# High and low log decays in one operand, and a new fixed order for the first tile of a three-stage kernel

## The chip, the cores and the metric

The kernel runs on one core of a Trainium2 chip. The metric is the device time of one execution in microseconds. The engines are PE (TensorE, matrix products; PEld is its loading of weights), DVE (VectorE), ACT (ScalarE), POOL (GpSimd) and SP (SyncE, which here issues every DMA).

## What is computed

A decaying linear attention over 4 x 8 heads and 768 positions in chunks, then two feed-forward stages on its 3072 x 256 output:

```python
log_a = np.log(np.clip(a, 1e-06, 1.0))
for c in range(nc):                                   # chunks
    cum = np.cumsum(la, axis=-1)
    L = np.exp(cum[:, :, :, None] - cum[:, :, None, :]) * causal
    M = np.einsum('bhin,bhjn->bhij', Cc, Bc) * L
    y[:, :, sl] = einsum(M, xc) + einsum(Cc, state) * exp(cum)
    state = exp(sum(la)) * state + sum_j(Bc[j] xc[j] * decay_from_j)
x = attn.transpose(0, 2, 1, 3).reshape(3072, 256)
x = (np.maximum(x @ w_in, 0.0) ** 2) @ w_out          # 256 -> 2048 -> 256
y = ((x @ w1) * (x @ w2) @ w3) @ w_out2               # 256 -> 1024 -> 1024 -> 256
```

The inputs are float32 (the weights arrive as 64-bit words that hold float64).

## The kernel before

The 3072 tokens are cut into six tiles of 512. Phase A of a tile is the first feed-forward stage (16 steps: `h_mm`, ReLU, square, `x2_mm`), phase B the second (8 steps). A value that enters a product of full accuracy is split into a high part, rounded to float32r, and a low part, the rest (`split`: ACT casts, DVE subtracts, L141 and L144), and a product is made of three passes over the parts.

**Weights.** A weight piece of 512 KB is fetched by `conv_load` (`ua0`, `ua1`, ... for the first stage) and converted: `conv_words` on ACT (L196, L198), `conv_bits` on DVE (L207, L210), `conv_parts` a cast on ACT for the first three pieces (L230) and on POOL for the others (L228), with the low part on DVE (L141). In the first tile's phase A one piece is converted in each of the 16 steps.

**Attention.** Chunks of 96 positions come in units of two. Units 0 to 2 (chunks 0 to 5), which the first tile needs, are computed in `startup()`, in an order written out by hand; every engine keeps it. For them `unit_g0` makes C.B on PE (L620), `unit_e1` the log decays as products of a selecting operand `pick` with `e_first` (L652), on top of a mask product (L646), and ACT takes their exponential (L656); `unit_m0` multiplies the two on DVE (L664). `state` and `value` are products on PE (L702, L740), and their results go over ACT and DVE to `xb` of the next chunk and to `xt`, the first tile's operand. From unit 3 on, `unit_split` splits B and C on ACT and DVE and writes them to DRAM (`hl_d`), and `unit_bc` reads them back in another layout with twelve DMAs (`bt`, `cb`).

**e_first** holds the cumulated log decays of the first two batches, for four kinds of chunk, in 32-row blocks. It is made by `decays_e_first` from the log decays `lp` and two shifted copies `lp2`, and kept as a high and a low half: every pick is made of two products, one per half, accumulated in PSUM. Four pick products follow each mask product.

**Order.** `startup()` runs under `in_order`, which ties each instruction to the one before it on its engine. Behind it a scheduler places the instructions of phase A and B. DMAs go out on SP in the order of the program, and SP waits in that order: a DMA that must wait holds back the ones behind it.

Of the kernel before, what the change touches and what calls it, by code (L numbers as in the profile page):

```python
# [15 lines left out]
P = 128  # L16
# [32 lines left out]
WARM = 2  # L49
TMPB = 6  # L50
# [3 lines left out]
PAD_ACT = (1, 2)  # L54
# [4 lines left out]
def kernel(  # L59
# [226 lines left out]
    lp2 = lps[:, 192:256].rearrange("p (v c) -> p v c", v=2)  # L286

    def constants():
        def diagonal(v):
            nc.gpsimd.affine_select(  # L290
                out=v, in_=v, pattern=[[0, v.shape[1]], [-1, v.shape[2]]], base=0, channel_multiplier=1,
                compare_op=ALU.not_equal, fill=1.0,
            )
# [5 lines left out]
        nc.vector.memset(lp2, 0.0)  # L299
        raw = [new_tmp()[:, :P] for _ in range(2)]  # L300
        nc.gpsimd.memset(raw[0], 0.0)
        diagonal(raw[0].unsqueeze(1))
        nc.gpsimd.memset(raw[1][:, :CH], 0.0)
        causal(raw[1][:, :CH].unsqueeze(1), NEVER)
        for k, eng in enumerate((nc.vector, nc.gpsimd)):
            eng.tensor_copy(
                pick[k].rearrange("r h (p j) -> r h p j", p=4),
                raw[0].rearrange("r (p k h) -> r k h p", p=4, k=4)[:, k].unsqueeze(3).to_broadcast([P, H, 4, 32]),
            )
        nc.vector.tensor_copy(ident, raw[0])  # L310
        nc.vector.tensor_copy(nmask, raw[1][:, :CH])
        nc.gpsimd.memset(id2, 0.0)
        for p in range(4):
            diagonal(id2[32 * p:32 * p + 32].unsqueeze(1))
        nc.gpsimd.memset(idc, 0.0)
        diagonal(idc[96:128])
        nc.gpsimd.memset(bt[64:96, :, :, CH:].bitcast(F32), 0.0)
# [10 lines left out]
    def decays_ln():  # L328
# [958 lines left out]
```

## Time and profile before

| | us |
|---|---|
| runs, median (lowest to highest) | 575.24 (574.53 to 681.34) |
| the profiled execution, its own time | 575.9 |
| its span in the trace | 574.2 |
| PE busy | 555.4 (97%) |
| DVE busy | 359.4 (63%) |
| ACT busy | 291.2 (51%) |
| POOL busy | 86.5 (15%) |

The shares are means over the whole span; the first 107 us look different from the rest. The trace gives for each instruction its start and duration, its line, what it writes and reads, and the idle time of its engine just before it with what ended that. A count such as x4 merges neighbours of one kind; where a merged row covers instructions that overlap, its duration is that of the whole group.

### The profile page before, as it was taken

The page shows a single profiled execution, that of the slowest core. Times are in us where ns is not written, and L with a number is a line of the kernel's source. Part 1 is how long each engine was busy: PE and PEld are TensorE (multiplying, and loading weights), DVE is VectorE, ACT ScalarE, POOL GpSimd, SP SyncE. Part 2 cuts the span into 40 slices and gives each one's busy share as a digit, 9 for nine tenths or more (in the row PEclk, how much of TensorE's full clock was granted, in tenths as well). Part 3 has the DMA queues.
Part 4 walks back from the last instruction along what each step waited for, and adds up shares of the span by engine and source line. Part 5 has one row for each costly group of instructions (what it writes and reads, how often), then busy time and mean ns, then how long its engine had stood idle before and what let it go on. Part 6 is the DMA issues. An engine that isn't in the chain of part 4 may idle for free.

```text
span 574.2 us, 9685 instructions
## 1 busy us (share of the span) xinstructions
PE 555.4 (97%) x3612; PEld 466.1 (81%) x3612; DVE 359.4 (63%) x647; ACT 291.2 (51%) x560; POOL 86.5 (15%) x134
## 2 busy tenths in 40 slices
PE   8878889999999999999999999999999999999997
PEld 6666667788888888888888888888888888888886
DVE  5558989888899675455766455665466574544431
ACT  6659776878887333352533353433454242534332
POOL 6315652000000304003012004020003020000000
PEclk9978999999999999999999999999999999999999
DMA  8268878034254635028241037220063220100001
GB/s 238 66 198 269 240 238 346 1 111 156 71 182 148 160 112 142 1 87 196 82 113 56 1 116 179 61 77 2 8 171 87 82 70 1 38 1 1 0 2 37
DMA packets 48735, 59.49 MB, mean 104 GB/s; under 512 B 22960, under 2 KB 36784, under 8 KB 48688
## 3 DMA queue, kind: packets, MB, share of 16 engines
q1 hardware_dynamic: 48688, 58.88, 35.4%
q8 instruction: 28, 0.46, 0.3%
q14 instruction: 19, 0.16, 0.1%
HBM read 50.20 MB, written 8.65 MB: 103 GB/s over the span
## 4 chain that ended last, share of the span: by engine, by line
PE 84%; DMA 8%; DVE 3%; ACT 2%; SPq 2%; issue 1%; DVEq 0%; ACTq 0%
PE mm L804 42%; PE acc L851 19%; PE acc L904 12%; PE mm L257 4%; DMA ua<-in_w_dram 3%; PE y L740 2%; SPq L93 2%; DMA hl_d<-gp 2%; PE g L601 2%; DMA uo<-in_w_dram 1%; PE y L702 1%; PE mm L652 1%; DMA hl_d<-hl 1%; DMA u<-in_w_dram 1%; PE mm L646 1%
## 5 line engine op out<-in xcount | busy, mean ns | idle before, releaser
L804 PE MATMUL mm<-xt,wa 128*128 128x512 f32 x576 | 150.5, 399 | 3.9 <-DVE wa L141 2.3
L834 ACT CAST gp<-tmp 128x512 fp32r<-128x512 f32 x144 | 89.4, 621 | 114.7 <-DVE tmp L892 62.7
L851 PE MATMUL acc<-gp,wa 128*128 128x512 f32 x576 | 146.0, 392 | 0.7 <-DVE gp L141 0.4
L804 PE MATMUL mm<-x,w 128*128 128x512 f32 x576 | 142.6, 393 | 0.0
L141 DVE TENSOR_TENSOR gp<-tmp,gp 128x512 fp32r<-128x512 f32 x144 | 101.5, 705 | 64.2 <-ACT gp L834 63.7
L804 PEld LDWEIGHTS mm<-xt,wa 128*128 128x128 f32 x576 | 106.8, 192 | 28.0 <-DVE wa L141 4.5
L851 PEld LDWEIGHTS acc<-gp,wa 128*128 128x128 f32 x576 | 106.4, 188 | 24.1 <-DVE gp L141 1.8
L804 PEld LDWEIGHTS mm<-x,w 128*128 128x128 f32 x576 | 104.5, 188 | 20.4 <-ACT tmp L884 0.2
L818 ACT ACTIVATE tmp<-mm 128x512 f32<-128x512 f32 x96 | 57.1, 596 | 55.7 <-PE mm L804 55.4
L904 PEld LDWEIGHTS acc<-w3o,gp 128*128 128x128 f32 x576 | 75.9, 190 | 4.8 <-DVE gp L141 0.5
L904 PE MATMUL acc<-w3o,gp 128*128 128x256 f32 x576 | 78.7, 283 | 0.1
L828 DVE TENSOR_TENSOR tmp<-tmp 128x512 f32<-128x512 f32 x68 | 47.3, 697 | 29.8 <-ACT tmp L818 29.4
L892 DVE TENSOR_TENSOR tmp<-tmp,mm 128x512 f32<-128x512 f32 x48 | 32.9, 686 | 48.3 <-PE mm L804 45.5
L536 POOL TENSOR_SCALAR_AFFINE_SELECT e<-e 96x768 f32<-96x768 f32 x26 | 26.2, 1019 | 238.9 <-DMA e<-e_d 135.1
L884 ACT COPY tmp<-mm 128x512 f32<-128x512 f32 x48 | 28.2, 587 | 46.3 <-PE mm L804 45.9
L555 POOL TENSOR_TENSOR xb<-xb,dec 96x256 f32<-96x256 f32 x32 | 22.7, 708 | 100.7 <-DMA xb<-in_xb_dram 44.2
L607 DVE TENSOR_TENSOR e<-g,e 128x384 f32<-128x384 f32 x52 | 27.7, 551 | 7.6 <-PE g L601 4.5
L257 PE MATMUL mm<-wo,w 128*128 128x256 f32 x128 | 23.7, 284 | 0.4 <-DVE w L141 0.4
L730 DVE SCALAR_TENSOR_TENSOR xb<-xb,through,y 32x64 f32<-32x64 f32 x72 | 20.4, 283 | 3.2 <-PE y L702 1.5
L257 PEld LDWEIGHTS mm<-wo,w 128*128 128x128 f32 x128 | 20.6, 191 | 2.0 <-DVE w L141 1.0
L207 DVE SCALAR_TENSOR_TENSOR cvs<-cvs,ua 128x512 uint32<-128x512 uint32 x16 | 13.1, 820 | 10.3 <-ACT ua L198 10.2
L601 PEld LDWEIGHTS g<-cb,bt 96*128 96x128 f32 x96 | 16.0, 190 | 2.6
(111 smaller groups left out, 462.4 us busy)
## 6 DMA issues: line engine op xcount, KB each, us to landing
u<-in_w_dram SPq DMA_DIRECT2D x24, 512.0 KB, 4.3
ua<-in_w_dram SPq DMA_DIRECT2D x16, 512.0 KB, 7.2
e<-e_d SPq DMA_DIRECT2D x40, 192.0 KB, 5.3
xb<-in_xb_dram SPq DMA_DIRECT2D x32, 192.0 KB, 4.3
bt<-hl_d SPq DMA_DIRECT2D x78, 48.0 KB, 2.0
hl_d<-gp SPq DMA_DIRECT2D x9, 384.0 KB, 2.5
cb<-hl_d SPq DMA_DIRECT2D x66, 48.0 KB, 2.0
out_dram<-tmp SPq DMA_DIRECT2D x10, 256.0 KB, 2.6
```

Of the source, the lines that this page charges most:

```text
L141: return nc.vector.tensor_tensor(out=lo, in0=src, in1=hi.bitcast(F32), op=ALU.subtract)
L257: nc.tensor.matmul(acc[:, :DM], v[:, l, e % 4 * P:(e % 4 + 1) * P], wo2[1 + e // 2][r][:, e % 2 * DM:(e % 2 + 1) * DM], start=(n == 0), st ...
L601: nc.tensor.matmul(ps[:, 2 * pp:2 * pp + 2], w, un["c2"][:, pr, :, j * CH:(j + 1) * CH], start=True, stop=True)
L607: nc.vector.tensor_tensor(out=m, in0=ps, in1=m, op=ALU.mult)
L804: i = nc.tensor.matmul(ps, w[m][:, l, col + k * P:col + (k + 1) * P], rhs[k][:, r, :], start=((l, r, k) == (1, 0, 0)), stop=((l, r, k) == ...
L818: nc.scalar.activation(r, ps, AF.Relu)
L828: nc.vector.tensor_tensor(out=g32, in0=r, in1=r, op=ALU.mult)
L834: nc.scalar.copy(g[:, 0, :], d[k])
L851: i = nc.tensor.matmul(acc["x2", t][e], wa[m][:, l, 256 + e * P:256 + (e + 1) * P], g[:, r, :], start=(m == 0 and n == 0), stop=(m == MF - ...
L884: nc.scalar.copy(s, ps)
L892: nc.vector.tensor_tensor(out=p32, in0=prods[t, m], in1=ps, op=ALU.mult)
L904: i = nc.tensor.matmul(acc["o"][sub // per][:, sub % per, :], g[:, l, sub * P:(sub + 1) * P], w3o[m // 2][:, r, m % 2, :], start=(m == 0 a ...
```

## The change

1. `lp4` takes the place of `lp2`: for each kind of chunk the 16 columns of log decays stand twice, side by side. `decays_e_first` then gives every row twice. The copies are two on ACT and four on DVE (before: four on ACT).
2. `e_first` is one 128-row operand: in the first of the two sets of rows minus the high part, in the other minus the low part. A `scalar_tensor_tensor` makes it in one operation from the rounded copy `e_hi` and PSUM, with the 0/1 column `halves[:, 1]` as the factor. `pick` selects both rows with -1. So a pick is one product.
3. The warm-up products read a 128-column fill and a broadcast column; `cb` is zeroed on POOL instead of DVE; the pick operands and constants come in another order. The pads of units 0 and 2 are on DVE (before: unit 0 alone), the copies into `bi` all on DVE.
4. `startup()` has another order. Unit 3 is split right behind the first two pick groups of unit 1, and weight 3 is loaded in the first block, weight 4 right behind unit 3's write.

```diff
-    lp2 = lps[:, 192:256].rearrange("p (v c) -> p v c", v=2)
+    lp4 = lps[:, 192:320].rearrange("p (v d c) -> p v d c", v=4, d=2)
...
-        warm = gp.tile([P, 512], F32, tag="gp", name="warm")
-        nc.vector.memset(warm, 0.0)
+        zero = gp.tile([P, P], F32, tag="gp", name="zero")
+        nc.vector.memset(zero, 0.0)
         for _ in range(WARM):
-            nc.tensor.matmul(y_bank, warm[:, :P], warm, start=True, stop=True, skip_group_check=True)
+            nc.tensor.matmul(
+                y_bank, zero, zero[:, :1].to_broadcast([P, 512]), start=True, stop=True, skip_group_check=True
+            )
...
+        nc.gpsimd.memset(cb.bitcast(F32), 0.0)
+        nc.gpsimd.memset(raw[:, :192 + CH], 0.0)
+        for base in (0, -16):
+            diagonal(sel, base, 32, -1.0)
...
+        def put(copy, v, r, r_in, k):
+            copy(lp4[r, v], lp[r_in, k, :2 * H].unsqueeze(1).to_broadcast([r.stop - r.start, 2, 2 * H]))
+
+        put(nc.scalar.copy, 0, slice(0, P), slice(0, P), 0)
+        put(nc.scalar.copy, 3, slice(0, P), slice(0, P), 2)
         for v, r, k, r_in in ((0, 64, 1, 0), (0, 32, 0, 96), (1, 0, 1, 64), (1, 64, 2, 0)):
             n = 32 if r == 32 or k == 2 else 64
-            nc.scalar.copy(lp2[r:r + n, v], lp[r_in:r_in + n, k, :4 * H])
+            put(nc.vector.tensor_copy, v + 1, slice(r, r + n), slice(r_in, r_in + n), k)
...
-        nc.scalar.copy(e_first[:, 0], pv)
-        nc.vector.tensor_tensor(out=e_first[:, 1], in0=pv, in1=e_first[:, 0].bitcast(F32), op=ALU.subtract)
+        hi = wts.tile([P, 4, CH], F32R, tag="wa11", name="e_hi")
+        nc.scalar.copy(hi, pv)
+        nc.vector.scalar_tensor_tensor(
+            out=e_first, in0=hi.bitcast(F32), scalar=halves[:, 1:2], in1=pv, op0=ALU.mult, op1=ALU.subtract
+        )
...
-            if u in PAD_ACT:
+            if u not in PAD_DVE:
...
         for h in range(2):
-            for l in range(2):
-                nc.tensor.matmul(
-                    ph[:, h], pick[k][:, 2 * q + h], e_first[:, l, v:v + 2], start=(not mask and l == 0), stop=(l == 1),
-                    skip_group_check=True,
-                )
+            nc.tensor.matmul(
+                ph[:, h], pick[k][:, 2 * q + h], e_first[:, v:v + 2], start=not mask, stop=True, skip_group_check=True
+            )
...
         unit_e1(1, 1)
-        conv_words(0)
-        conv_bits(0)
+        unit_split(3, "w120")
+        unit_rows(bt)
+        state(1)
+        chunk_pre(3)
         value(0)
...
+        conv_load(1)
+        unit_bc(3)
```

On SP, from the seventeenth DMA on, before the change (`raw` are a unit's operands, `ua` the weights, `hl_d3` and `hl_d4` the split operands of units 3 and 4 in DRAM, `xb` a chunk):

```order
L93 DMA raw_133<-in_raw_dram 128x2x192
L93 DMA ua2_135<-in_w_dram 128x1024
L93 DMA hl_d3_478<-hl_473 128x2x384
L93 DMA ua3_481<-in_w_dram 128x1024
L93 DMA raw_483<-in_raw_dram 128x2x64
L93 DMA raw_483<-in_raw_dram 128x2x32
L93 DMA bt_90<-hl_d3_478 32x4x96 x6
L93 DMA cb_91<-hl_d3_478 16x4x192 x6
L93 DMA xb_514<-in_xb_dram 96x512
L93 DMA ua4_516<-in_w_dram 128x1024
L93 DMA hl_d4_538<-hl_533 128x2x384
```

and at the same place with the change:

```order
L93 DMA ua2_133<-in_w_dram 128x1024
L93 DMA raw_135<-in_raw_dram 128x2x192
L93 DMA ua3_137<-in_w_dram 128x1024
L93 DMA hl_d3_328<-hl_323 128x2x384
L93 DMA ua4_392<-in_w_dram 128x1024
L93 DMA bt_90<-hl_d3_328 32x4x96 x6
L93 DMA cb_91<-hl_d3_328 16x4x192 x6
L93 DMA xb_493<-in_xb_dram 96x512
L93 DMA ua5_495<-in_w_dram 128x1024
L93 DMA raw_497<-in_raw_dram 128x2x64
L93 DMA raw_497<-in_raw_dram 128x2x32
L93 DMA hl_d4_508<-hl_503 128x2x384
```

Weight 3 now stands ahead of unit 3's write and weight 4 ahead of the twelve reads. From the thirtieth DMA on the two orders are alike.

On DVE, from the decay products of unit 0 (`e<-g,e`) to those of unit 2, before the change (`cvs` and `wa` are the conversion of weight 0, `xt` the low part of a value, `hl` that of unit 3's split):

```order
L664 TENSOR_TENSOR e<-g,e 128x2x192 x4
L207 SCALAR_TENSOR_TENSOR cvs<-cvs,ua_121 128x512
L210 SCALAR_TENSOR_TENSOR cvs<-ua_121,cvs 128x512
L141 TENSOR_TENSOR xt<-mm,xt 128x2x96
L664 TENSOR_TENSOR e<-g,e 128x2x192 x4
L141 TENSOR_TENSOR xt<-mm,xt 128x2x96 x2
L141 TENSOR_TENSOR wa_462<-cvs,wa_462 128x512
L664 TENSOR_TENSOR e<-g,e 128x2x192 x4
L141 TENSOR_TENSOR hl<-raw_111,hl 128x192
```

and with the change (L679 is the line of the decay products, L602 that of the pads):

```order
L679 TENSOR_TENSOR e<-g,e 128x2x192 x4
L141 TENSOR_TENSOR hl<-raw_111,hl 128x192
L141 TENSOR_TENSOR hl<-raw_113,hl 128x192
L141 TENSOR_TENSOR xt<-mm,xt 128x2x96
L602 TENSOR_SCALAR cp<-raw_113,halves 128x192 x2
L141 TENSOR_TENSOR xt<-mm,xt 128x2x96
L679 TENSOR_TENSOR e<-g,e 128x2x192 x4
L207 SCALAR_TENSOR_TENSOR cvs<-cvs,ua_121 128x512
L210 SCALAR_TENSOR_TENSOR cvs<-ua_121,cvs 128x512
L141 TENSOR_TENSOR xt<-mm,xt 128x2x96 x2
L679 TENSOR_TENSOR e<-g,e 128x2x192 x4
```

Unit 3's split and two pads moved ahead of the decay products of unit 1, where now two values stand instead of one; ahead of those of unit 2 the low part of weight 0 is gone.

## Rows read from the trace of the kernel before

**Rows 1.** Stretches: us; busy PE, PEld, DVE, ACT, POOL; clock; DMA; GB/s.
```profile
20.00:25.00 5.00, 4.53 (x76) 3.64 (x74) 0.67 (x2) 3.26 (x9) 1.75 (x4) 1.00 0.00 0
52.00:80.00 28.00, 25.40 (x148) 19.05 (x147) 27.95 (x42) 20.53 (x42) 19.52 (x23) 1.00 0.74 202
80.00:92.00 12.00, 9.42 (x61) 6.64 (x59) 9.04 (x19) 8.85 (x19) 4.38 (x6) 1.00 1.00 355
107.00:574.00 467.00, 462.82 (x2843) 395.01 (x2842) 278.50 (x503) 215.49 (x399) 42.26 (x60) 1.00 0.28 78
```

**Rows 2.** Chain that ended last: start, us, engine, tile, line, count.
```profile
8.31 0.38 PE mm L646
8.69 0.42 PE mm L652 x4
9.11 0.20 PE mm L646
...
10.36 0.86 PE g L620 x16
...
12.65 0.56 PE y L702 x8
...
14.01 0.47 PE mm L740 x16
```

**Rows 3.** Timeline of PE: start, us, line, operands, count [idle before <-releaser].
```profile
26.93 1.40 PE L740 MATMUL mm<-e,xb 128*32 128x96 f32 x32 [2.40 <-DVE e L664]
...
30.04 2.93 PE L804 MATMUL mm<-xt,wa 128*128 128x512 f32 x6 [0.94 <-ACT xt L144]
...
44.51 0.69 PE L652 MATMUL mm<-e_first,pick 128*128 128x192 f32 x4 [3.55 <-ACT e L656]
45.03 4.54 PE L804 MATMUL mm<-xt,wa 128*128 128x512 f32 x12
...
50.79 1.52 PE L804 MATMUL mm<-xt,wa 128*128 128x512 f32 x6
```

**Rows 4.** Timeline of DVE.
```profile
25.30 1.94 DVE L664 TENSOR_TENSOR e<-g,e 128x384 f32<-128x384 f32 x4
```

**Rows 5.** Timeline of ACT.
```profile
23.66 0.49 ACT L656 ACTIVATE e<-mm 128x384 f32<-128x384 f32 x1 [0.43 <-PE mm L652]
...
27.97 0.32 ACT L144 CAST xt<-mm 128x192 fp32r<-128x192 f32 x1 [1.90 <-PE mm L740]
...
29.29 0.59 ACT L144 CAST hl<-raw 128x192 fp32r<-128x192 f32 x2
...
35.52 0.59 ACT L818 ACTIVATE tmp<-mm 128x512 f32<-128x512 f32 x1
...
38.75 0.60 ACT L818 ACTIVATE tmp<-mm 128x512 f32<-128x512 f32 x1 [0.70 <-PE mm L804]
42.58 0.66 ACT L196 ACTIVATE cvs<-ua 128x512 f32<-128x512 f32 x1 [3.23 <-DMA ua<-in_w_dram]
```

**Rows 6.** Timeline of SP's queue of DMA issues.
```profile
27.80 0.39 SPq L93 DMA_DIRECT2D hl_d<-hl x1
...
32.42 2.72 SPq L93 DMA_DIRECT2D bt<-hl_d x6
...
38.57 0.43 SPq L93 DMA_DIRECT2D ua<-in_w_dram x1
```

**Rows 7.** Line 207 from 28 to 110 us: ns min/median/max, first and last start.
```profile
L207 DVE SCALAR_TENSOR_TENSOR cvs<-cvs,ua x15: 677/693/1358, 29.4 to 88.6; 128x512 uint32<-128x512 uint32 x15
```

**Rows 8.** DVE by line and shape, 0 to 30 us: busy us, mean ns | idle.
```profile
L141 DVE TENSOR_TENSOR xt<-mm,xt 128x192 fp32r<-128x192 f32 x5 | 1.8, 352 | 1.5 <-ACT xt L144 1.5
...
L296 DVE MEMSET warm<- 128x512 f32 x1 | 0.5, 485 | 1.0 <-PEq L1273 1.0
```

**Rows 9.** One-microsecond stretches of PE: us, busy, clock, DMA, GB/s.
```profile
28.00:29.00 1.00, 1.00 (x20) 0.52 0.27 100
...
45.00:46.00 1.00, 1.00 (x5) 0.55 1.05 315
```

More of the change, by code (lines that the diff above doesn't have):

```diff
@@ L49 @@
 WARM = 2
+PAD_DVE = (0, 2)
 TMPB = 6
@@ new lines, in constants @@
+        nc.vector.memset(lp4, 0.0)
+        raw = new_tmp()
+        sel, one, low = raw[:, :64].rearrange("r (p c) -> r p c", p=4), raw[:, 64:192], raw[:, 192:192 + CH]
+        nc.gpsimd.memset(cb.bitcast(F32), 0.0)
+        nc.gpsimd.memset(raw[:, :192 + CH], 0.0)
+        for base in (0, -16):
+            diagonal(sel, base, 32, -1.0)
+        diagonal(one.unsqueeze(1), 0, 0)
+        causal(low.unsqueeze(1), NEVER)
+        nc.gpsimd.memset(id2, 0.0)
+        for p in range(4):
+            diagonal(id2[32 * p:32 * p + 32].unsqueeze(1), 0, 0)
@@ L311, in constants, with rounded @@
[L311 to L317, printed above, removed]
+        def rounded():
+            nc.vector.tensor_copy(ident, one)
+            nc.vector.tensor_copy(nmask, low)
+        return picks, rounded
     def decays_load(k):
@@ L385, in decays_e @@
         e_rows[w] = e
-    e_first = wts.tile([P, 2, 4, CH], F32R, tag="w127", name="e_first")
+    halves = const.tile([P, 2], F32, name="halves")
+    e_first = wts.tile([P, 4, CH], F32R, tag="w127", name="e_first")
     def decays_e_first():
@@ L572 @@
     cps = {}
-    halves = const.tile([P, 2], F32, name="halves")
     def unit_pad(u):
@@ L1044, in value, with m0 @@
             chunk_out(g, ys[g])
+        def m0(u):
+            for q in range(4):
+                unit_m0(u, q)
         decays_load(0)
@@ L1061, in startup @@
         chunk_xb(5, "w126")
+        conv_load(1)
         unit_load(4)
         conv_load(1)
-        constants()
+        picks, rounded = constants()
         decays_ln()
-        nc.vector.memset(cb.bitcast(F32), 0.0)
-        decays_e_first()
+        picks(0, nc.vector)
+        rounded()
         nc.vector.tensor_reduce(
@@ L1070, in startup @@
         )
+        decays_e_first()
+        picks(1, nc.gpsimd)
         nc.vector.tensor_copy(bi[:, :, CH:], id2.unsqueeze(1).to_broadcast([P, FIRST[1], 32]))
@@ L1075, in startup @@
         chunk_pre(0)
+        for q in range(4):
+            unit_e1(0, q)
+        unit_g0(0)
         chunk_pre(1)
-        unit_e1(0, 0)
-        unit_e1(0, 1)
-        unit_e1(0, 2)
-        unit_g0(0)
-        unit_e1(0, 3)
-        for q in range(4):
-            unit_m0(0, q)
         unit_bi(2, 6)
         unit_pad(1)
+        state(0)
         chunk_pre(2)
+        m0(0)
         unit_e1(1, 0)
-        state(0)
         unit_e1(1, 1)
-        conv_words(0)
-        conv_bits(0)
+        unit_split(3, "w120")
+        unit_rows(bt)
+        state(1)
+        chunk_pre(3)
         value(0)
+        unit_pad(2)
         unit_e1(1, 2)
         unit_g0(1)
-        state(1)
         unit_e1(1, 3)
-        chunk_pre(3)
-        for q in range(4):
-            unit_m0(1, q)
         value(1)
+        m0(1)
+        conv_load(1)
+        unit_bc(3)
+        state(2)
+        chunk_pre(4)
+        conv_words(0)
         unit_e1(2, 0)
-        unit_pad(2)
-        state(2)
         unit_e1(2, 1)
-        chunk_pre(4)
+        conv_bits(0)
         value(2)
+        state(3)
+        chunk_pre(5)
+        unit_e1(2, 2)
         unit_g0(2)
-        unit_e1(2, 2)
-        state(3)
         unit_e1(2, 3)
-        conv_parts(0)
-        chunk_pre(5)
-        for q in range(4):
-            unit_m0(2, q)
-        unit_split(3, "w120")
-        unit_rows(bt)
-        conv_load(1)
-        unit_load(5)
-        unit_bc(3)
         value(3)
+        m0(2)
         state(4)
@@ L1123, in startup @@
         conv_load(1)
+        unit_load(5)
+        conv_parts(0)
+        unit_split(4, "w121")
         value(4)
+        chunk_xb(7)
+        conv_load(1)
         conv_words(1)
-        conv_bits(1)
-        unit_split(4, "w121")
-        chunk_xb(7)
-        conv_load(2)
         value(5)
         state(5)
+        conv_bits(1)
         chunk_xb(8)
```

26 lines of the change are left out of this document (10 added, 16 removed).

## The prediction

> **What bounds the kernel now.** I read the table by stretches first [rows 1]. From 107 us to the end PE is busy for 462.8 of 467 us at the full clock, and there the change leaves the order of every engine as it was: a microsecond gained or lost before that point is gained or lost at the end. The question is when the program reaches it. From 52 to 80 us DVE is the full engine (27.95 of 28 us); from 80 to 92 it is busy for 9.04 of 12 us and the DMA engines are at 1.00.
>
> Then I read the timelines of PE, DVE, ACT and SP up to 52 us [rows 3 to 6] for one long wait and followed it back. PE stands still for 3.55 us before 44.51, since ACT has not emptied a PSUM buffer. ACT stands for 3.23 us before 42.58, since weight 4 has not landed. That piece was issued at 38.57, behind twelve reads of unit 3's split operands that begin at 32.42; those wait for the write issued at 27.80, once DVE had made the split. Meanwhile, from 20 to 25 us, the DMA engines moved nothing [rows 1]. A second, smaller loss is the stretch from 80 to 92, where DVE has 2.96 us without work and the DMA engines have none to spare.
>
> **Up to the first tile's first product,** which stands at 30.04 [rows 3]. I lay the new order end to end.
>
> (a) The fill ahead of the warm-up products shrinks from 512 columns, 0.485 us [rows 8], to 128; in proportion and with some fixed cost about 0.2 us is left, so PE starts 0.3 us sooner. Of the four ACT copies of log decays two stay and four go to DVE, and POOL zeroes `cb`: PE takes the decay products up when the warm-up ends, at about 5.0 us, without a wait, so all this costs nothing under the warm-up; uncovered it would cost at most 1 us. The pick groups then begin at 8.0 instead of 8.31 [rows 2].
>
> (b) A pick group is one mask product and four pick products: 0.38 + 0.42 us behind a product of another kind, 0.20 + 0.42 behind its like [rows 2]. Two of the four picks go, 0.21 us, in 12 groups 2.5 us; and only seven groups instead of ten stand behind another kind, 0.5 us more. A new wait stands against it. Up to value 1 PE has 8 groups (four of 0.59, four of 0.41), two C.B products of 0.86, two states of 0.56 and two values of 0.47 [rows 2]: 7.8 us, so value 1 ends at 15.8. ACT casts it (0.32 [rows 5]), DVE takes its low part (0.35 [rows 8]), and only behind that DVE makes the four decay products of unit 1 (1.94, as those of unit 2 [rows 4]): 18.4. PE, through with state 2 and two groups at 17.35, waits 1.05 us for them before value 2. The last group ends 0.3 + 3.0 - 1.05 = 2.2 us sooner, at 21.45.
>
> (c) DVE begins the decay products of unit 2 at 25.30 now [rows 4], 1.64 us after ACT began the last exponential at 23.66 [rows 5], because it takes the low part of weight 0 first. In the new order value 3 alone stands between: 0.47 on PE, 0.32 on ACT, 0.35 on DVE. They run from 22.6 to 24.5, and PE's next values start at 24.55 instead of 26.93 [rows 3], behind an idle of 2.0 us where it was 2.40.
>
> (d) From ACT's cast of value 4 at 27.97 to the first tile's product at 30.04 it takes 2.07 us, with unit 4's split casts (0.59) in between [rows 3, 5]; these come earlier now, which leaves 1.5. With value 4 itself, 0.47: first product at 26.6, **3.4 us sooner**. Ends: 2.0 (one more wait like that in (b)) and 4.0.
>
> **The transfers.** Unit 3's split casts come on ACT behind the first two groups of unit 1 now, so the split is done near 13.7 and written then, instead of at 27.80 [rows 6]. The first loads are through by 20 us at the latest [rows 1]; weight 3, now among them, and this write are 0.9 MB, 2.6 us at the 355 GB/s of the stretch with the full queue [rows 1]. So the write is through by 22 or so; the twelve reads and the next load took 6.15 us (32.42 to 38.57 [rows 6]), which brings SP to 28 where it was at 38.5: **10 us sooner**. Weight 4 is issued near 14 instead of 38.57 and lands before 25. What is queued behind the reads on SP (chunk 6, weight 5, unit 5's operands, unit 4's write) is wanted by no engine before 29.
>
> **First tile, up to 52 us.** I take ACT, where everything in this stretch stands in one row. Between its first ReLU at 35.52 and the words of weight 4 at 42.58 it has two waits, 0.70 for PE and 3.23 for the weight [rows 5], 3.9 us. Weight 4 is there by then, PE's second tile product is no longer waited for since four fewer picks stand ahead of it, and the first ReLU keeps its distance to the first product, 5.5 us, which ACT's own casts of weights 1 and 2 set. The eight picks fewer here lie under those waits. **3.9 us more, 7.3 together.** Ends: 3.2 (the 0.70 stays) and 5.4 (the lower clock behind the wait goes too, below).
>
> **52 to 80.** DVE is full and its work is the same, so the block moves as a whole: nothing. A cost is possible, since a weight step of DVE takes anything from 0.677 to 1.358 us in this tile [rows 7], and POOL is at work for 19.5 of these 28 us [rows 1]: an earlier start can push more of POOL's work beside DVE's. For some 60 operations at 0.05 us it is 3 us; from 0 to 3 I take 0, as the same pairs of operations stand side by side.
>
> **80 to 92.** DVE's idle time is 12 - 9.04 = 2.96 us, for the last weights of this tile and the first of the next matrix. SP is 10 us ahead of its old times and the engines 7.3, so the fetches lead by 2.7 us more than now. That could take nearly all of it, but what waited together will not all fit. I take **2.2**, ends 0 and 3.0.
>
> **Sum.** 3.4 + 3.9 + 2.2 = 9.5 us. The profiled execution took 575.9 us (span 574.2, 1.7 around it): 566.4. The median of the runs, 575.24, stands 0.7 below that execution, which would give 565.7. I say **566.0**.
>
> **PE's clock.** The granted clock is 0.52 in the second from 28 us, behind the idle of 2.40, and 0.55 in that from 45 us, behind the 3.55 [rows 3, 9]: the 1.2 GHz level. The first costs nothing now, as ACT's casts set the first ReLU; in the second twelve products took 4.54 us where six take 1.52 at the full rate [rows 3], so 1.5 us. The change leaves 2.0 us of idle at the first place, and I leave that fall in the sum as it is. The Trainium skill ("TensorE: Matmul & The Clock Gate", "Why this matters for your kernels") says that an idle gap between bursts of products brings the engine back to the lower rate. By that rule, the trace agrees, with 0.52 and 0.55 behind the two idles; it speaks against the change, which breaks PE's row in the front at one more place, and the third rival is what it would do here.
>
> **Rivals.** First, *only the front is gained*: in the first tile DVE and POOL, which share the casts of each weight, wait on each other where they waited for the DMA, and the 3.9 us come back. For it: DVE is full as soon as weights flow [rows 1]. Against it: ACT's two waits have no DVE in them. 575.2 - 3.4 = 572; 17%.
>
> Second, *all transfer waits go* and the second fall of the clock with them: 3.4 + 5.4 + 3.0 = 11.8, with the upper end of the front 12.4: 563; 25%. For it: SP's lead of 10 us. Against it: DVE's full stretch follows at once.
>
> Third, *slower, by the clock*: PE's row between 17 and 45 us has waits of 1.05, 2.0 and 0.6 us, and then a stretch in which ACT hands out one PSUM buffer at a time. If the clock is at half from 18 us on, some 7 us of work before the tile and 12 in it take twice as long, 19 us more, of which ACT's row may hide 6. It decides from 9.5 us on; with 13 the time is 575.2 - 9.5 + 13 = 579. For it: the two falls above. Against it: from 20 to 25 us, with PE at 4.53 of 5, the clock was full [rows 1]. 5%.
>
> Fourth, *no gain*: the split on ACT and DVE in the front delays the later chunks by as much as the picks spare, and DVE takes the rest: 574 to 577; 4%. The forecast (564 to 569.5) holds the other 49%.
>
> **Numbers.** A measurement of this kernel can tell about 2%, 11.5 us, from no change; faster is below 563.7. The second rival, with the forecast's lower edge, gives 0.26; slower begins at 586.7, which only the third rival could reach: 0.03; the rest is 0.71. The range goes from 562.0 (the good ends of all terms, 12.4) to 572.7 (the first rival), each with the 0.7 by which the two undisturbed runs differ.
>
> **What would show it.** PE's first tile product near 26.6; a wait of about 1 us before value 2; unit 3's write issued near 14 and SP through with the twelve reads near 28; weight 4's words on ACT without a wait; less than 1 us of DVE idle before the last weight of the tile. Wrong would be: that write landing after 25 us; waits of ACT for weight 5 or 6 of over 1 us; a clock near 0.5 for more than 8 us up to 45; weight steps of DVE that take over 1 us in the mean.

## The result, and the profile after

| | before | after |
|---|---|---|
| runs, median (us) | 574.88 | 565.5 |
| the profiled execution, its own time | 575.9 | 566.51 |
| its span in the trace | 574.2 | 564.8 |
| PE busy | 555.4 | 549.2 |
| first product of the first tile | 30.04 | 27.02 |
| DVE's low part of weight 5 (counted from 0) | 52.56 | 42.47 |
| first tile's result leaves PSUM (DVE's first `x<-acc`) | 103.10 | 92.97 |

The ratio is 0.985, interval 0.983 to 0.987 (it leaves out the one slow execution of the kernel before, 681.34 us): some 9 us less, which is under the 2% that the prediction took as the bound of what can be told. On the chip of the later runs the changed kernel took 566.6 beside 574.08 (0.988, 0.985 to 0.990). Executions of one kernel lie up to 6 us apart there (571.65 to 577.70 for the kernel before, 15 runs), so below, medians less than about 1.5 us apart count as not told apart, and one profiled execution can stand 2 us beside its kernel's median.

PE's timeline in the changed kernel (start, us, line, operands, count, idle before and what ended it; L755 are the values, L819 the tile's first products):

```profile
17.94 0.90 PE L755 MATMUL mm<-e,xb 128*32 128x96 f32 x16 [0.91 <-DVE e L679]
...
24.07 1.97 PE L755 MATMUL mm<-e,xb 128*32 128x96 f32 x32 [1.88 <-DVE e L679]
...
27.02 1.87 PE L819 MATMUL mm<-xt,wa 128*128 128x512 f32 x6 [0.17 <-ACT xt L144]
...
33.13 0.85 PE L668 MATMUL mm<-e_first,pick 128*128 128x192 f32 x4 [2.18 <-ACT tmp L833]
```

They answer to [rows 3]: a new wait of 0.91 us before value 2; an idle of 1.88 instead of 2.40 before values 4 and 5; the first tile product 3.02 us sooner. The wait of 3.55 us before 44.51 is gone. The 2.18 us before 33.13, for ACT's first ReLU, stand at another place, where the kernel before waited for 0.24:

```profile
36.17 1.14 PE L652 MATMUL mm<-e_first,pick 128*128 128x192 f32 x8 [0.24 <-ACT tmp L818]
```

DVE makes the decay products of unit 2 2.86 us sooner than in [rows 4]:

```profile
22.44 1.94 DVE L679 TENSOR_TENSOR e<-g,e 128x384 f32<-128x384 f32 x4
```

ACT's timeline, beside [rows 5]:

```profile
32.49 0.59 ACT L833 ACTIVATE tmp<-mm 128x512 f32<-128x512 f32 x1
...
34.24 0.69 ACT L196 ACTIVATE cvs<-ua 128x512 f32<-128x512 f32 x1
...
58.84 0.62 ACT L849 CAST gp<-tmp 128x512 fp32r<-128x512 f32 x1 [3.25 <-DMA hl_d<-gp]
```

The first ReLU (L833) stands 3.03 us sooner, and weight 4's words (L196, 34.24) come without the wait of 3.23. But the row at 58.84 is new: ACT wants to write a `gp` tile in which unit 5's split operands still lie, as their write to DRAM (`hl_d`) has not landed. SP's queue of DMA issues, beside [rows 6]:

```profile
13.52 0.38 SPq L93 DMA_DIRECT2D hl_d<-hl  x1
...
21.55 2.71 SPq L93 DMA_DIRECT2D bt<-hl_d  x6
...
27.59 0.43 SPq L93 DMA_DIRECT2D ua<-in_w_dram  x1
...
49.85 1.75 SPq L93 DMA_DIRECT2D hl_d<-gp  x2
...
58.48 1.28 SPq L93 DMA_DIRECT2D bt<-hl_d  x3
```

Unit 3's write goes at 13.52 (27.80 before), its reads begin at 21.55 (32.42), the next weight goes at 27.59 (38.57): SP is 11 us ahead. Unit 5's write (two DMAs of 96 KB, x2) is issued from 49.85, and its reads can begin only at 58.48. The view of the DMAs gives the size and the median time from issue to landing: first these two before the change, then the same two after it, then all eight of this size in the program with the change.

```profile
hl_d<-gp SPq DMA_DIRECT2D x2, 96.0 KB, 9.1
...
hl_d<-gp SPq DMA_DIRECT2D x2, 96.0 KB, 8.5
...
hl_d<-gp SPq DMA_DIRECT2D x8, 96.0 KB, 1.9
```

The two writes were as slow before the change, but there only SP's reads waited for them and no engine that computes. The other transfers issued from 49 to 53 us took as long here (two weight pieces 8.8, a chunk 7.6).

The stretches (columns as in [rows 1]):

```profile
26.00:48.00 22.00, 19.34 (x115) 15.37 (x111) 17.48 (x26) 20.03 (x44) 9.23 (x12) 0.89 0.80 237
48.00:60.00 12.00, 10.07 (x68) 8.23 (x69) 10.23 (x21) 8.75 (x19) 6.37 (x11) 1.00 0.83 258
60.00:74.00 14.00, 13.98 (x99) 10.83 (x98) 14.00 (x23) 13.05 (x26) 9.35 (x11) 1.00 0.81 254
74.00:86.00 12.00, 10.79 (x68) 8.47 (x67) 12.00 (x21) 7.56 (x14) 4.95 (x7) 1.00 1.00 396
97.00:564.70 467.70, 462.58 (x2842) 395.08 (x2842) 278.78 (x502) 215.09 (x398) 41.57 (x60) 1.00 0.28 78
```

ACT is nearly full from 26 to 48 (20.03 of 22). From 48 to 60 every engine has gaps, most of them around the wait at 58.84. From 60 to 86 DVE is busy for all of 26 us; the 2.96 us that it lacked work between 80 and 92 [rows 1] are gone. (In a second execution, under "The changed kernel again", it lacks work for 2.6 of these 26 us.) From 97 on PE works as it did from 107 before [rows 1]. DVE's step on a weight (L207) has the same durations as in [rows 7]:

```profile
L207 DVE SCALAR_TENSOR_TENSOR cvs<-cvs,ua x14: 676/682/1356, 30.5 to 77.8; 128x512 uint32<-128x512 uint32 x14
```

Followed by DVE's low parts of the weights, after minus before, the lead is 3.1 us at weight 1, 2.1 at weight 3, 7.4 at weight 4, 10.1 at weight 5, 8.7 at weight 8 (56.88 against 65.63), 8.1 at weight 9 (61.99 against 70.06), 10.0 at weight 15, and 9.4 at the end of the span. For weights 5 to 7 this is no even measure: in DVE's order weight 5 stands behind two low parts of the tile itself now (`gp<-tmp`), where three stood ahead of it before the change. ACT's square of each of the 16 steps is an even one. Steps 4, 8 and 16, first before the change and then after it:

```profile
53.13 0.63 ACT L826 ACTIVATE tmp<-tmp 128x512 f32<-128x512 f32 x1
...
65.98 0.63 ACT L826 ACTIVATE tmp<-tmp 128x512 f32<-128x512 f32 x1
...
98.90 0.64 ACT L826 ACTIVATE tmp<-tmp 128x512 f32<-128x512 f32 x1
```

```profile
45.77 0.63 ACT L841 ACTIVATE tmp<-tmp 128x512 f32<-128x512 f32 x1
...
60.49 0.62 ACT L841 ACTIVATE tmp<-tmp 128x512 f32<-128x512 f32 x1
...
88.50 0.64 ACT L841 ACTIVATE tmp<-tmp 128x512 f32<-128x512 f32 x1
```

Step 8 is the one behind the wait at 58.84. The same lead, in us, for this and four of the kernels below:

| step | 1 | 4 | 8 | 10 | 16 |
|---|---|---|---|---|---|
| changed | 3.0 | 7.4 | 5.5 | 8.2 | 10.4 |
| changed again | 4.2 | 8.5 | 5.1 | 7.0 | 9.2 |
| order alone | 1.6 | 5.9 | 3.2 | 5.1 | 8.5 |
| decay products first | 5.8 | 9.4 | 6.1 | 7.0 | 9.9 |
| 24 idle products | 0.7 | 5.0 | 5.4 | 7.4 | 8.8 |

### The profile page after: what moved, and what is told of

Same layout as the page of the kernel before. It is cut to its first block, busy times and chain, and to the rows that moved or that the text cites. A ratio compares the mean times of both kernels' runs of the same rounds, so it can differ in the third digit from the quotient of the medians.

```text
span 564.8 us, 9623 instructions
## 1 busy us (share of the span) xinstructions
PE 549.2 (97%) x3580; PEld 462.5 (82%) x3580; DVE 358.6 (63%) x653; ACT 289.7 (51%) x555; POOL 87.2 (15%) x136
## 4 chain that ended last, share of the span: by engine, by line
PE 81%; DVE 5%; issue 4%; DMA 4%; ACT 3%; SPq 2%; POOL 1%; DVEq 0%; ACTq 0%; POOLq 0%
PE mm L819 41%; PE acc L866 19%; PE acc L919 11%; PE mm L257 4%; DMA ua<-in_w_dram 2%; DMA hl_d<-gp 2%; SPq L93 2%; PE y L755 1%; PE g L618 1%; DMA u<-in_w_dram 1%; PE y L717 1%; DVE gp L141 1%; DVE cvs L207 1%; PE y L298 1%; DVE cvs L210 1%
## 5 line engine op out<-in xcount | busy, mean ns | idle before, releaser
L819 PE MATMUL mm<-xt,wa 128*128 128x512 f32 x576 | 148.5, 396 | 2.3 <-DVE wa L141 1.5
L141 DVE TENSOR_TENSOR gp<-tmp,gp 128x512 fp32r<-128x512 f32 x144 | 103.1, 716 | 64.3 <-ACT gp L849 63.9
L819 PE MATMUL mm<-x,w 128*128 128x512 f32 x576 | 142.6, 394 | 0.0
L819 PEld LDWEIGHTS mm<-xt,wa 128*128 128x128 f32 x576 | 106.0, 190 | 25.0 <-DVE wa L141 2.6
L819 PEld LDWEIGHTS mm<-x,w 128*128 128x128 f32 x576 | 104.6, 188 | 20.4 <-ACT tmp L899 0.3
L833 ACT ACTIVATE tmp<-mm 128x512 f32<-128x512 f32 x96 | 57.3, 596 | 56.6 <-PE mm L819 56.4
L257 PE MATMUL mm<-wo2l,w 128*128 128x256 f32 x64 | 18.1, 283 | 0.0
```

The source lines that it names most:

```text
L141: return nc.vector.tensor_tensor(out=lo, in0=src, in1=hi.bitcast(F32), op=ALU.subtract)
L257: nc.tensor.matmul(acc[:, :DM], v[:, l, e % 4 * P:(e % 4 + 1) * P], wo2[1 + e // 2][r][:, e % 2 * DM:(e % 2 + 1) * DM], start=(n == 0), st ...
L819: i = nc.tensor.matmul(ps, w[m][:, l, col + k * P:col + (k + 1) * P], rhs[k][:, r, :], start=((l, r, k) == (1, 0, 0)), stop=((l, r, k) == ...
L833: nc.scalar.activation(r, ps, AF.Relu)
```

## The experiments

Ratios are against the kernel before on the same chip. The last three columns are from the profiled execution (us; for the kernel before the one shown ahead of the prediction): first product of the tile, DVE's low part of weight 5, and the first read of unit 5's split on SP.

| kernel | median us (lowest to highest) | ratio (interval) | product | weight 5 | reads |
|---|---|---|---|---|---|
| before | 573.96 (571.61 to 575.87) | | 30.04 | 52.56 | 70.07 |
| picks alone | 573.16 (572.08 to 573.95) | 0.999 (0.998 to 1.001) | 28.32 | 49.77 | 65.36 |
| order alone | 566.92 (565.52 to 568.0) | 0.988 (0.986 to 0.990) | 28.47 | 43.90 | 60.68 |
| changed, split late | 568.56 (567.64 to 569.74) | 0.990 (0.988 to 0.992) | 26.79 | 45.19 | 66.18 |
| changed, fetches late | 565.97 (565.48 to 568.56) | 0.987 (0.985 to 0.990) | 26.07 | 41.49 | 59.72 |
| changed again | 566.6 (566.08 to 568.8) | 0.988 (0.985 to 0.990) | 25.91 | 41.30 | 58.77 |
| own tile for unit 5 | 566.09 (564.56 to 568.19) | 0.987 (0.984 to 0.989) | 27.31 | 42.74 | 58.99 |
| casts 1, 2 on POOL | 566.39 (565.59 to 568.45) | 0.987 (0.985 to 0.990) | 27.36 | 45.52 | 61.24 |
| decay products first | 566.99 (566.05 to 568.13) | 0.988 (0.985 to 0.990) | 24.30 | 39.74 | 57.91 |
| all three | 571.04 (568.22 to 575.03) | 0.995 (0.992 to 0.998) | 25.18 | 45.91 | 59.40 |
| 24 idle products | 566.85 (565.05 to 568.92) | 0.988 (0.985 to 0.991) | 29.39 | 44.82 | 58.56 |
| 8 idle products | 568.12 (565.53 to 570.53) | 0.990 (0.987 to 0.994) | 26.28 | 41.70 | 57.78 |
| six low parts fewer | 564.85 (563.86 to 566.25) | 0.984 (0.981 to 0.987) | 26.79 | 42.20 | 59.36 |

The first five stood on one chip, the next four beside a kernel before of 574.08, the last four beside 573.99.

### The parts alone

**Picks alone**: the changed kernel with the order of the kernel before.

```diff
         unit_e1(1, 1)
-        unit_split(3, "w120")
-        unit_rows(bt)
-        state(1)
-        chunk_pre(3)
+        conv_words(0)
+        conv_bits(0)
         value(0)
...
+        conv_parts(0)
+        chunk_pre(5)
+        for q in range(4):
+            unit_m0(2, q)
+        unit_split(3, "w120")
```

> The changed kernel with the old order of the front: the doubled operand, one pick product instead of two and the short fill stay; unit 3's split, the weight fetches, the pads and the copies into bi stand where they stood before. Theory (front and transfers are separate terms): only the front is gained, 0.3 us for the fill and 2.5 for the 24 pick products, and the write, the twelve reads and weight 4 follow it in the same chain as before, so the wait of ACT for weight 4 stays at about 3.2 us: 572.3 us, 2.6 less than before. Rival one (the transfers set the pace from 28 us on and the front is hidden): within 0.5 us of before. Rival two (the shorter picks carry the whole gain): 566.

The median is 0.8 us below that of the kernel before, and the ratio's interval takes in 1: not told apart from nothing. PE's rows:

```profile
16.46 0.45 PE L664 MATMUL mm<-nmask,ident 128*128 128x384 f32 x1 [0.74 <-DVE xt L141]
...
25.00 1.84 PE L756 MATMUL mm<-e,xb 128*32 128x96 f32 x32 [2.40 <-DVE e L680]
```

From the first pick group to the first tile product it takes 21.4 us (6.93 to 28.32), in the kernel before 21.8 (8.24 to 30.04). PE works for 1.9 us less in this stretch (16.45 against 18.32) and stands idle for 1.5 more: of the four new waits, 1.7 us together, the longest is 0.74 for DVE before 16.46, and the 2.40 before 25.00 are as they were.

**Order alone**: the kernel before, with two products per pick, in the new order.

```diff
         unit_e1(1, 1)
-        conv_words(0)
-        conv_bits(0)
+        unit_split(3, "w120")
+        unit_rows(bt)
+        state(1)
+        chunk_pre(3)
         value(0)
```

> The kernel before with the new order of the front alone: unit 3 split behind the first two pick groups of unit 1, weights 3 and 4 fetched sooner, pads and bi copies as in the change; every pick is still two products and cb is zeroed on DVE. Theory: the front keeps only the 0.5 us of the fewer changes of kind and loses the 1.0 us wait, so the tile's first product stands near 29.9; the transfers are early all the same and ACT's waits before weight 4 go (3.9 us), with some 1.5 to 2.2 from 80 us on: 568.5 us, 6 to 6.5 less than before. Rival (both parts are needed for either gain): 572 to 575. Rival (the order carries all of it): 565.5.

Seven microseconds are gained by the order without the picks. Its front is as long as with the picks alone, 21.4 us (7.06 to 28.47); with both together it is 19.2 (7.79 to 27.02 in the changed kernel).

**Split late**: the changed kernel with the early fetches, but unit 3's split behind the decay products of unit 2.

```diff
-        unit_split(3, "w120")
-        unit_rows(bt)
         state(1)
...
         m0(2)
+        unit_split(3, "w120")
+        unit_rows(bt)
+        unit_bc(3)
```

> The changed kernel with unit 3's split, its write and its twelve reads put back behind the decay products of unit 2; weights 3 and 4 are still fetched in front of them. Theory (the place of the split sets when SP is free): weight 4 is there, but weight 5 is issued behind the twelve reads, near 38 us, so ACT's wait moves from weight 4 to weight 5 and most of the 3.9 us comes back: 569.5 to 571. Rival (the two early weight fetches are what helps): 565.5 to 566.5, as the changed kernel.

ACT waits for the weights behind the reads now, at 38.18 and further on (1.37 us before 43.03), where the changed kernel has no such wait:

```profile
38.18 0.67 ACT L196 ACTIVATE cvs<-ua 128x512 f32<-128x512 f32 x1 [0.90 <-DMA ua<-in_w_dram]
...
79.36 0.68 ACT L196 ACTIVATE cvs<-ua 128x512 f32<-128x512 f32 x1 [2.39 <-DMA ua<-in_w_dram]
```

**Fetches late**: the early split, with the fetches of weights 3 and 4 where they were.

```diff
         chunk_xb(5, "w126")
-        conv_load(1)
         unit_load(4)
...
-        conv_load(1)
+        conv_load(2)
         conv_words(1)
```

> The changed kernel with the order of the fetches before the change: weight 3 behind unit 3's write, weight 4 behind the twelve reads and chunk 6, weights 5 and 6 behind chunk 7; the split stays early. Theory: SP is through with the twelve reads near 27, weight 4 lands near 32 and is wanted by ACT at 34.2, so nothing is lost: 565.5, within 0.7 us of the changed kernel; weight 5 or 6 may be late by up to 1 us. Rival (the early weight fetches are what helps): 568.5 to 569.5.

The early split does without the early fetches, since SP is through with the twelve reads at 26.1. With the fetches early and the split late 5.4 us of the gain are left (the picks and the rest of the new order are in both kernels), and with the split early the fetches add nothing that can be told: the two moves take the same wait away.

### Waits within the first tile

**The changed kernel again**, as a base on this chip.

> The changed kernel again, as the yardstick for the next three on the same chip: 0.984 to 0.988 of before, about 565 us.

```profile
23.28 1.32 PE L755 MATMUL mm<-e,xb 128*32 128x96 f32 x32 [1.88 <-DVE e L679]
```

```profile
59.23 0.62 ACT L849 CAST gp<-tmp 128x512 fp32r<-128x512 f32 x1 [4.77 <-DMA hl_d<-gp]
```

```profile
75.40 0.43 DVE L206 TENSOR_SCALAR uo<-uo 128x512 uint32<-128x512 uint32 x1 [2.37 <-DMA uo<-in_w_dram]
```

The first product stands 1.1 us sooner than in the other profile of this same kernel, and the wait for the write-out is 1.5 us longer. And DVE is not busy throughout from 60 to 86 us: it waits for 2.37 us for a weight of the next matrix (`uo`), which in the first profile it did not.

**Own tile**: unit 5's split gets a tile that no one waits for.

```diff
-        put(ph, 7, unit_split, 5)
+        put(ph, 7, unit_split, 5, "w122")
```

> The changed kernel with unit 5's split in a tile of its own (the place w122, free by then) instead of one of the four gp tiles. In the changed kernel ACT stands 3.25 us before 58.84 for the next gp tile, which is still being written out to DRAM (8.6 us behind the weights), and PE stands 1.93 us behind it. Theory (this wait took the place of the transfer waits that went, it gives back part of the gain): it goes, 1.5 to 2 us less than the changed kernel. Rival (DVE is the full engine around it and only refills): within 0.5 us of the changed kernel.

ACT's wait near 59 is gone and DVE fills up in its place:

```profile
48.00:60.00 12.00, 12.00 (x80) 10.09 (x79) 12.00 (x24) 11.93 (x27) 5.72 (x7) 1.00 0.86 270
60.00:74.00 14.00, 13.01 (x86) 9.54 (x85) 14.00 (x21) 10.48 (x20) 11.19 (x15) 0.88 0.77 247
74.00:86.00 12.00, 12.00 (x75) 9.75 (x75) 12.00 (x21) 8.30 (x17) 5.97 (x7) 1.00 1.02 399
```

DVE is busy for 38 of 38 us; of 3.25 us spared on ACT, half a microsecond is left in the median, not told apart from none.

**Casts on POOL**: those of weights 1 and 2 too.

```diff
-        if kind == "a" and j > 2:
+        if kind == "a" and j > 0:
```

> The changed kernel with the casts of weights 1 and 2 on POOL, which does nothing from 24 to 34.8 us, instead of ACT. In the changed kernel ACT waits 1.11 and 0.42 us for DVE's bits of these weights before each cast, with the first ReLU queued behind, and PE stands 2.18 us before 33.13 for that ReLU. Theory (the first ReLU is set by ACT's row, not by PE or its clock): the first ReLU comes 2 to 2.7 us sooner; from there ACT is the full engine (20.0 of 22 us to 48) and has 1.1 us less to do: 1.5 to 2.5 us less than the changed kernel. Rival (DVE's low parts wait for POOL's casts and the whole row keeps its pace): within 0.5 us.

Nothing again; ACT meets a wait of 1.97 us for the same write-out, before 61.64.

**Decay products first**: those of units 1 and 2 ahead of values 1 and 3.

```diff
-        value(1)
         m0(1)
+        value(1)
...
-        value(3)
         m0(2)
+        value(3)
```

> The changed kernel with DVE's decay products of units 1 and 2 ahead of the low parts of values 1 and 3, which in the changed kernel stand in front of them. Theory (these low parts are the new wait of PE before value 2 and lengthen the one before value 4): both waits of PE, 0.91 and 1.88 us, shrink by 0.5 to 0.6 each, the tile's first product comes about 1 us sooner, and as ACT's row follows it the end too: 0.5 to 1 us less than the changed kernel. Rival (ACT's exponentials and casts set this part): within 0.3 us.

```profile
58.26 0.62 ACT L849 CAST gp<-tmp 128x512 fp32r<-128x512 f32 x1 [4.73 <-DMA hl_d<-gp]
```

The first product (24.30) is 1.6 to 2.7 us sooner than in the two profiles of the changed kernel, and ACT waits 4.73 us for the write-out: it stands at 58.26 all the same, and the median is not lower.

**All three edits** together.

> The changed kernel with all three of the single edits at once: unit 5's split in a tile of its own, the casts of weights 1 and 2 on POOL, the decay products of units 1 and 2 ahead of the values. Each alone moved the median by half a microsecond or less. Theory that each wait only handed the row over to the next one (ACT's row up to 48 us, the wait for the write-out at 58, DVE afterwards): together they bring about 2 us, 564.5 where the changed kernel took 566.6. Rival, that between 60 and 97 us DVE and the transfers set the pace whatever is spared before: 566 to 567, with the last weight's low part still near 84.8 us.

Slower than the changed kernel by 4.4 us, and the two intervals do not meet. The last weight's low part stands at 83.8, 1 us sooner than in the changed kernel; the time goes later:

```profile
93.23 0.54 PE L755 MATMUL y<-e,xb 128*32 128x96 f32 x16 [2.09 <-DVE e L624]
...
97.21 5.63 PE L819 MATMUL mm<-xt,wa 128*128 128x512 f32 x15 [0.40 <-ACT xt L144]
```

```profile
97.00:98.00 1.00, 0.79 (x2) 0.70 (x3) 1.00 (x2) 0.15 (x1) 0.00 (x0) 0.50 0.00 0
100.00:101.00 1.00, 1.00 (x4) 0.81 (x3) 0.00 (x0) 0.00 (x0) 0.00 (x0) 0.50 0.00 0
```

PE waits 2.09 us for DVE's decay products (`e`), and behind that the clock is at 0.50 up to 101 us, and fifteen tile products take 5.63 us (3.68 in the changed kernel). ACT's sixteenth square, at 88.0, is still 10.9 us ahead of the kernel before, and the first of the next tile, at 103.1, is 4.3 ahead: all that is lost is lost between these two. On DVE the order of many rows differs from that of the changed kernel, as the scheduler places the later pieces otherwise once the casts are elsewhere (with the casts on POOL alone it does so too, and the time is the same); which of these moves costs it was not tried.

### What takes the front's gain

**24 idle products** ahead of values 4 and 5.

```diff
         state(4)
+        fill = new_mm()[:, :4 * CH].rearrange("p (n i) -> p n i", n=4)
+        for _ in range(24):
+            nc.tensor.matmul(
+                fill, ident, nmask.unsqueeze(1).to_broadcast([P, 4, CH]), start=True, stop=True, skip_group_check=True
+            )
         chunk_xb(6)
```

> The changed kernel with 24 products of no use (mask product's form, 0.20 us each behind their like) ahead of values 4 and 5, where PE stands idle for 1.88 us: 4.8 us of work, so the first tile's product comes 2.3 us (if the clock stays full and the values take 1.32 instead of 1.97 us) to 2.9 us later, while SP's transfers stay where they are. Theory that a microsecond of the front is one at the end: 569 to 569.5. Rival, that the first tile further on waits for DVE and the transfers and takes the front's time up: under 567.5. The picks alone and the order alone came out 1.5 us apart in the front and not in the medians, and this tells whether that can be.

```profile
22.70 4.58 PE L1139 MATMUL mm<-nmask,ident 128*128 128x384 f32 x24
```

```profile
58.93 0.62 ACT L849 CAST gp<-tmp 128x512 fp32r<-128x512 f32 x1 [0.97 <-DMA hl_d<-gp]
```

```profile
51.49 0.99 SPq L93 DMA_DIRECT2D hl_d<-gp  x2
...
58.56 1.28 SPq L93 DMA_DIRECT2D bt<-hl_d  x3
```

The first product (29.39) is 2.4 us later than in the first profile of the changed kernel, and so is DVE's low part of every weight from 1 to 8 (weight 8: 59.23 against 56.88). Then ACT's wait for the write-out has shrunk from 3.25 to 0.97 us, and it ends where it ended, as unit 5's write lands at 58.5 whether issued at 49.85 or 51.49: at step 4 ACT's lead is 2.4 us less than in the first profile of the changed kernel, at step 8 0.1 less. At step 16 it is 1.6 less than in that profile and 0.4 less than in the second one, so further on nothing can be told from two executions. The median is 0.25 us above that of the changed kernel; the interval of its ratio ends at 0.991, where 2.4 us more would have given 0.992.

**8 idle products**: the same with `range(8)`.

> As the kernel with 24 products of no use, but with 8 of them: 1.6 us, which fit into PE's idle time of 1.88 us before values 4 and 5. Theory that the fall of the clock to 0.50 there costs: the clock stays at 1.00 up to 28 us, the two values take 1.32 instead of 1.97 us, the first tile's product comes 0.6 us sooner, and the time is 0.6 us less, 566.0. Rival, that ACT's row hides it: the first ReLU stands where it stood, and the time is 566.6. If the clock falls all the same, a little later, what held it up was not the idle time alone.

```profile
23.74 1.24 PE L755 MATMUL mm<-e,xb 128*32 128x96 f32 x32 [0.25 <-DVE e L679]
...
32.39 1.17 PE L668 MATMUL mm<-e_first,pick 128*128 128x192 f32 x4 [2.39 <-ACT tmp L833]
```

```profile
27.00:28.00 1.00, 1.00 (x7) 0.55 (x7) 0.78 (x2) 0.10 (x1) 0.00 (x0) 1.00 0.05 6
33.00:34.00 1.00, 1.00 (x5) 0.90 (x5) 0.85 (x2) 1.00 (x3) 0.00 (x0) 0.50 0.99 285
```

The clock holds over the front and the two values take 1.24 us instead of 1.97; it falls behind the next wait instead, 2.39 us for ACT. But in the second profile of the changed kernel, without these products, the values took 1.32 us at the full clock too, so that the products held it up is not shown. The time is not below 566.6, and its six runs lie 5 us apart: inconclusive on whether it is slower.

**Six low parts fewer** on DVE.

```diff
+        if kind == "a" and 9 <= j <= 14:
+            KEPT[kind][j] = HiOnly(w, wa[8])
+            return
         split_lo(w[:, 0, :], w[:, 1, :], v)
```

> The changed kernel without the low parts of weights 9 to 14: six DVE subtractions between 60 and 84 us are left out, and the products of these weights read weight 8's low part in their place, so that PE has as much to do. In the changed kernel DVE is busy for all of the 26 us from 60 to 86, and the DMA engines are at 1.00 from 74 to 86. Theory that DVE sets the pace there: six times 0.69 us or more go, the first tile's result leaves PSUM 4 us sooner and the time is about 562.5. Rival, that the transfers of the last weights set it: DVE gets idle time that a DMA ends, and the time is 565.5 to 566.5.

```profile
60.45 0.69 DVE L141 TENSOR_TENSOR gp<-tmp,gp 128x512 fp32r<-128x512 f32 x1 [3.00 <-ACT gp L859]
...
77.43 0.43 DVE L206 TENSOR_SCALAR uo<-uo 128x512 uint32<-128x512 uint32 x1 [2.43 <-DMA uo<-in_w_dram]
```

```profile
60.00:74.00 14.00, 13.53 (x69) 10.81 (x70) 11.72 (x19) 12.07 (x23) 9.17 (x12) 0.88 0.50 165
74.00:86.00 12.00, 12.00 (x93) 9.39 (x93) 8.81 (x16) 8.58 (x18) 3.39 (x6) 1.00 1.02 372
```

The median is 1.75 us below that of the changed kernel, for some 4 us of DVE's work: between the two theories. DVE is without work for 5.5 us of these 26, and the two longest waits in or just ahead of them end with the write-out of unit 5's split (3.00, by way of ACT) and with a weight of the next matrix (2.43). Nearly the same two waits stand in the second profile of the changed kernel (3.32 and 2.37), so they are not the edit's doing. That less work on DVE makes the time shorter shows that DVE sets the pace in part; the transfers set it in part too, in some executions without any edit.

## Why the prediction was right, and where it was not

**The sum** was 566.0 and the median is 565.5 (566.6 on the other chip). Its terms were not all what they were called.

**Front, as a place: right, but for one term.** First product 3.02 us sooner instead of 3.4. (b): wait before value 2 0.91 instead of 1.05. (c): decay products at 22.44 instead of 22.6, values at 24.07 instead of 24.55, idle 1.88 instead of 2.0. (d) was short: I put value 4 at 0.47 us, PE's time for it alone, though [rows 3, 5] have 1.04 from its start to ACT's cast (26.93 to 27.97), with the granted clock at 1.00; it was 1.04 again in the second profile of the changed kernel (23.28 to 24.32) and 1.37 in the first (24.07 to 25.44), where the clock is 0.56 from 24 to 25. With the smaller fill PE's first product starts at 1.13 instead of 1.53, 0.4 sooner for the 0.3 forecast, but the pick groups don't follow it: they begin at 7.79 in one profile of the changed kernel, at 6.95 in the other, and at 7.06 with the order alone, which has the old fill.

**Front, as a term of the sum: wrong.** 3.4 us were added as if they reached the end. In the changed kernel they do not: 2.4 us more in the front cost 0.25 in the median, and 1.6 to 2.7 less brought nothing. The leads on ACT show where it goes: from 5.0 to 9.4 us at step 4 with the same order of the transfers (24 idle products, the two profiles of the changed kernel, decay products first), they are 5.4, 5.5, 5.1 and 6.1 at step 8, behind the write-out. The picks alone, in the order of before, bring at most 1.4 (the lower end of their ratio). The step that failed is the one that took the first tile's block to move as a whole behind the front: ACT's row is held at 58 us by a write that does not come sooner with the front (its reads go at 58.56, 58.48, 58.77 and 57.91 in these four).

**Transfers: right.** Write issued at 13.52 (14), reads from 21.55 (22), SP through at 27.1 (28), weight 4 at 14.11 and without a wait on ACT.

**First tile up to 52 us: right, on the row it was read from.** 7.3 us were forecast at this point, and ACT's squares of steps 3 to 6 are 7.3 to 7.4 us sooner (step 4: 45.77 against 53.13). In the second profile it is 8.5, with 1.1 of it already there at the first product. Weight 5's low part on DVE came 10.1 sooner, but it stands one step of the tile earlier in DVE's order. ACT's row was the right one to read: the order, which takes its waits away, brings 7 us without the picks, and with only one of its two moves the kernel keeps 5.4 or 8.0.

**52 to 80: wrong in how, near in size.** "The block moves as a whole" did not hold: the lead on ACT fell from 7.4 us at step 4 to 5.5 at step 8, behind the 3.25 us that it waits for unit 5's write-out, and was 8.2 again at step 10 (66.91 against 75.13). In the second profile it fell from 8.5 to 5.1 and came back to 7.0. So the net is 0.8 more in one and 1.5 less in the other, where 0 was forecast: that it came out near nothing is luck. No rival had this wait; the first comes near it in its effect, but there DVE and POOL were to wait on each other, and here ACT, and DVE and PE behind it, wait for a DMA. The trace of before had the 9.1 us of that write, with no computing engine waiting for it; I followed the reads of unit 3 and not this write. DVE's steps did not grow (682 ns in the median, 693 before), so the cost that I bounded there, 0 to 3, was 0.

**80 to 92: right in size on ACT, not told on DVE.** From step 10 to step 16 ACT's lead grew by 2.2 us in both profiles, by 2.2 in the sum. On DVE, from weight 9 to weight 15, it is 2.0 in the first profile and 0.4 in the second (8.4 to 8.8). DVE had no idle time before the last weight in the first, and 2.6 us of it in the second.

So the terms, added up along ACT's row, come to the total (7.4, then 8.2, then 10.4, of which 9.4 are left at the end of the span), but they are not independent: with the front of the 24 idle products, 0.65 us sooner than before instead of 3.4, the same sum says about 568.8, and 566.85 was measured. That the sum came within 0.5 us is in part luck. That the gain has a ceiling is seen in the table: of the kernels with the early split and all of the work, the order alone, fetches late, changed again, own tile, decay products first and 24 idle products have weight 5 anywhere from 39.7 to 44.8 us, and their medians lie between 565.97 and 566.99. The 8 idle products (41.70 with 568.12) lie above, with executions 5 us apart. Where weight 5 comes later the time rises (45.19 with 568.56, 49.77 with 573.16), though not by that alone: with the casts on POOL it is 45.52 and the time 566.39.

**The clock** fell at two places again: to 0.50 from 24 to 27 us behind the idle of 1.88, and from 34 to 37 behind the 2.18. Before the change the first fall, behind the 2.40, lasted from 28 to 35 us.

```profile
26.00:27.00 1.00, 0.84 (x10) 0.60 (x6) 0.15 (x2) 0.96 (x3) 0.00 (x0) 0.50 0.40 112
...
35.00:36.00 1.00, 1.00 (x4) 0.62 (x2) 0.47 (x1) 1.00 (x3) 1.00 (x2) 0.50 1.02 238
```

That the first fall costs nothing agrees with the kernel with eight idle products, whose profile does not have it and whose time is not lower. The second fall, with 4.54 us for twelve products in the kernel before [rows 3], was left in the sum. The second one after the change (six products in 2.55 us from 33.89, 1.52 at the full rate) lasts as long; in the second profile of the same kernel there is none, and PE's wait at this place is 0.90.

**Rivals.** All transfer waits going (563) did not happen, as a new one came. Slower by the clock did not either: it was low for about 7 us up to 45, not from 18 us on, and before the change for about 7 us up to 45 as well.

What stays open: which of DVE's moves makes three edits that each leave the time alone cost 4.4 us together; how DVE's work and the transfers share the pace after 60 us, as two profiles of one kernel differ there; and how much of the front reaches the end, which six executions a kernel bound only loosely.

## What to carry to other kernels

Follow one transfer chain to its next link before you add a gain: here the reads of one unit came 11 us sooner, and the engines then waited for the write-out of a later unit, whose tile they wanted again. The profile before had that write at 9.1 us, though no computing engine waited for it yet. Gains at two places add up only if nothing between them comes at a time of its own, as that write did; idle work of a few microseconds at the earlier place shows whether the end moves with it. Two moves that take the same wait away are worth one. And follow a lead by instructions that stand in the same order in both kernels: by DVE's low part of weight 5 it was 10.1 us, by ACT's row 7.4.

## What the runs showed that was not expected

- Two writes of 96 KB took 8.5 us from issue to landing with the DMA engines at 0.88 (50 to 58.5 us), where the median of the eight writes of this size is 1.9. The Trainium skill ("DMA: Bandwidth & Descriptors", "Anatomy of one DMA — SWDGE (gpsimd) path") gives a fixed 2.0 us and 436 KB per us, for another issuing path than SP's; an estimate by this is 2.2 us. The median is near it, the two writes are not, and the measured time decides here.
- The same kernel shows the low clock at two places in one execution (24 to 27 and 34 to 37 us) and at one in another (26 to 29), with an idle of 1.88 us ahead of the first in both (in the second the clock falls only behind a further 0.90). That is execution to execution, not an effect of an edit. In the one profile with 0.25 in place of the 1.88 it stayed at 1.00 up to 32 us. The Trainium skill ("TensorE: Matmul & The Clock Gate", "Why this matters for your kernels") has idle gaps between bursts bring the lower rate, but speaks of longer ones; here 0.50 stands behind 1.88, 2.39 and 2.40 us, and the measurement decides.
- The same instructions of the start, up to the first pick group, end 0.8 us apart in two executions of one kernel (7.79 and 6.95), so a difference of that size in the front of two single profiles is no effect of an edit. With the same front as the changed kernel, own tile and casts on POOL took 20.5 and 20.9 us from the first pick group to the first tile product instead of 19.2; in both, PE stands idle for over 1.2 us before 12.6, and the profile names nothing that ended it.
